# Weight tiles of two modes to a transfer, and a re-ordered last stretch, in a sparse-attention and spectral-mix kernel

## The chip, the cores and the metric

The kernel runs on one core of one Trainium2 chip. The metric is the device time of one execution in microseconds, taken as the median of several runs. A profile is of one execution.

## What is computed

Two layers, one after the other. Attention: 8 batches, 8 heads, 576 rows of 64; the first four heads see a local window of 32 rows, the last four see rows of the same position modulo 32. Then a spectral mix over the rows of the attention's output x (8 x 576 x 512):

```
X = rfft(x, axis=1);  Xr, Xi = real and imaginary part of X[:, :64]
Yr = einsum('bmd,mde->bme', Xr, w_r) - einsum('bmd,mde->bme', Xi, w_i)
Yi = einsum('bmd,mde->bme', Xr, w_i) + einsum('bmd,mde->bme', Xi, w_r)
y = irfft(Y with its first 64 modes set to Yr + i*Yi, n=576, axis=1)
u = x + y
out = u + max(u @ w_ch, 0)
```

`w_r` and `w_i` are 64 x 512 x 512 each, all inputs are float32; each of the 64 modes has weights of its own.

## The kernel before

**Loads.** All of q, k, v, w_r, w_i and w_ch is loaded by POOL (GpSimd), with a cast to float16 in the transfer. POOL is a queue: its transfers are issued in the order of the program, each when the buffer that it writes is free, and at most eight are in flight, since a transfer waits for the landing of the one eight places before it. `w_fetch` (L175) loads the weights of a mode, half of the input channels at a time: part 0 (half 1) for modes 0 to 63, then part 1 (half 0) for modes 0 to 63. One such piece is a tile of 128 partitions x 4 x 512: w_r in partitions 0 to 63, w_i in 64 to 127 (mode 0 has no w_i). Each is a transfer of its own (L190). The pool `pw` has 11 tiles (`NWBUF`); six more pieces (`GUEST`, L169) sit in space that other tiles (X0, Y0, YT) take over later. `w_ch` takes one of the 11 (L197). `load_str` (L214) loads the rows of the strided heads of a batch: 64 partitions by a transfer for each of v, q, k, and for each even batch a small one with partitions 64 to 71 of two batches (L222). `load_loc` (L229) loads those of the local heads.

**Stages.** (1) Strided attention, batch by batch (L742), with loads and weight prefetch at the head of each batch. (2) Local attention (L770), with the 64 modes of part 0 (`mode(0, m)`) spread between its steps. (3) The 64 modes of part 1 (`mode(1, m)`, L837 and L948). `mode` (L532) is 16 matmuls with 16 columns, a weight tile as the stationary operand; after it `w_fetch` asks for the next piece. Beside the modes of part 1 there is a list `work` of 76 pieces: four `w_turn`, and for each batch four `turn` (L578: transposes of x) and five `premix` (L627: four matmuls with 512 columns, x @ w_ch, and four transposes back, with a copy by ACT, L650, and one by DVE, L651). Each `premix` leaves v0 = x @ w_ch and a copy xo of x. `spec` turns 16 finished modes of Y for four batches. (4) The tail: 36 units of 128 rows. `v_rows` (L888) adds irfft(Y) @ w_ch to v0 in PSUM and takes the relu by ACT into `rl` (L897); `u_rows` (L907) makes u, and DVE adds `rl` and writes `osb` (L916), from which SP's queue stores the output. `rl` and `osb` are tiles of `pw` too. `v_early` and `u_early` put v0 and xo into PSUM ahead of that, and `again(n)` (L944) is n matmuls whose result nobody reads.

**The order** of each engine's instructions is that of the program text (`manual_schedule`). In stage 3 the pieces are handed out by hand (L835-L846): with `LATE = 10`, 56 of them evenly beside modes 0 to 50, then two beside each of modes 51 to 60. Then come the early matmuls, and then modes 61, 62 and 63 with nothing between them:

```
for i in range(3):
    if i < 2:
        v_early(i)
    u_early(i)
warm = psum("v")
...
for m in range(NM - 3, NM):
    mode(1, m)
again(2)
spec_last(0)
again(3)
```

Of the kernel before, what the change touches and what calls it, by code (L numbers as in the profile page):

```python
# [10 lines left out]
FP = mybir.dt.float32  # L11
F16 = mybir.dt.float16
# [6 lines left out]
DM = 512  # L19
NM = 64  # L20
# [3 lines left out]
JG = [(0, 6), (6, 11), (11, 16)]  # L24
SCALE = float(1.0 / np.sqrt(D))
NEG = -30000.0
NWBUF = 11


def _host_consts():  # L30
# [49 lines left out]
def kernel(  # L80
# [10 lines left out]
    nc = tc.nc  # L91
# [3 lines left out]
    big = ctx.enter_context(tc.tile_pool(name="big", bufs=1))  # L95
# [5 lines left out]
    def psum_pools(**bufs):  # L101
        pctx.close()
        for n, c in bufs.items():
            pss[n] = pctx.enter_context(
                tc.tile_pool(name="ps_" + n, bufs=c, space=PSUM)
            )

    def psum(kind, half=False):
        if half:
            return pss[kind].tile([128, 1024], F16, tag=kind, name=kind)  # L110
        return pss[kind].tile([128, 512], FP, tag=kind, name=kind)
# [16 lines left out]
    def const_load(eng, *which):  # L128
        for n in which:
            eng.dma_start(cs[n][:, 0 : hosts[names.index(n)].shape[1]], drams[n])  # L130
# [13 lines left out]
    def spectra_tile(n):  # L144
        if n == "X0":
            Xh[0] = big.tile([128, 4, B, 2, NM], F16, tag=n, name=n)
        else:
            YS[n] = big.tile([128, 4, 4, 16, 16], F16, tag=n, name=n)

    xb = [px.tile([128, 11, 256], F16, tag="xb", name="xb") for _ in range(B)]  # L150

    pw = ctx.enter_context(tc.tile_pool(name="pw", bufs=NWBUF))
    actx = ctx.enter_context(ExitStack())
# [3 lines left out]
    ring = pat.tile([128, 12, 2048], F16, name="ring")  # L157
# [8 lines left out]

    GUEST = {3: ("Y0", 0), 4: ("Y0", 1), 5: ("X0", 0), 6: ("X0", 1)}  # L169
    GUEST |= {15: ("YT", 0), 16: ("YT", 1)}  # L170
    guests = {}
    w_tiles = []
    w_chs = {}

    def w_fetch(n=1):  # L175
        for _ in range(n):
            i = len(w_tiles)
            if i >= 2 * NM:
                return
            half, m = 1 - i // NM, i % NM  # L180
            if i in GUEST:
                n, j = GUEST[i]
                if j == 0:
                    guests[n] = big.tile([128, 2, 4, DM], F16, tag=n, name="wt")
                wt = guests[n][:, j]
            else:
                wt = pw.tile([128, 4, DM], F16, tag="w", name="wt")

            for ri, src in enumerate([moe_w_r, moe_w_i] if m else [moe_w_r]):
                nc.gpsimd.dma_start(  # L190
                    wt[ds(64 * ri, 64)],
                    src[m, ds(256 * half, 256), :].rearrange("(p c) e -> p c e", c=4),
                )
            w_tiles.append(wt)

    def w_ch_fetch():
        w_ch = pw.tile([128, 4, DM], F16, tag="w", name="w_ch")  # L197
        nc.gpsimd.dma_start(w_ch, moe_w_ch.rearrange("(c p) e -> p c e", p=128))
        w_chs["n"] = w_ch

# [3 lines left out]
    SRC = {2: v, 0: q, 1: k}  # L204
    SLOT = {2: 0, 0: 1, 1: 2}

    def str_in(b, vi):
        return ring[0:72, 3 * (b % 4) + SLOT[vi], :]
# [2 lines left out]
        t = ring[:, ds(2 * (b % 6), 2), :].rearrange("p n x -> p (n x)")  # L211
        return t[:, ds(1152 * vi, 1152)]

    def load_str(b):  # L214
        for vi in (2, 0, 1):
            nc.gpsimd.dma_start(
                str_in(b, vi)[0:64],
                SRC[vi][b, 4:8].rearrange("h (c r) d -> (h c) (r d)", r=32)[0:64],
            )
            if b % 2 == 0:  # L220
                n = 3 * (b % 4) + SLOT[vi]
                nc.gpsimd.dma_start(  # L222
                    ring[64:72, n : n + 4 : 3, :],
                    SRC[vi][b : b + 2, 4:8].rearrange(
                        "b h (c r) d -> (h c) b (r d)", r=32
                    )[64:72],
                )

    def load_loc(*bs):  # L229
        for b in bs:  # L230
# [301 lines left out]
    def mode(slot, m):  # L532
        half = 1 - slot
        mi, mg = m % 8, m // 8
        if mi == 0:
            ypt[slot] = psum("y")
        yp = ypt[slot]
        yv = yp.rearrange("p (m e x) -> p m e x", m=8, e=4)
        wt = w_tiles[slot * NM + m]
        pr = ds(0, 128 if m else 64)  # L540
        for e in range(4):
            for c in range(4):
                nc.tensor.matmul(  # L543
                    yv[:, mi, e, :],
                    wt[pr, XC[c], ds(128 * e, 128)],
                    Xh[half][pr, c, :, :, m],
                    start=(c == 0),
                    stop=(c == 3),
                )
        if slot or m not in GUEST:  # L550
            w_fetch()
        ends = {7: 8}
        if slot and mg == 7:
            ends = {5: 6, 7: 2}
        if mi in ends:
            n = ends[mi]
            m0 = mi + 1 - n
            part = (
                slice(None),
                slice(None),  # L560
                mg // 2,
                slice(None),
                ds(8 * (mg % 2) + m0, n),
            )
            src = yp.rearrange("p (m e x) -> p e x m", m=8, e=4)[:, :, :, ds(m0, n)]
            if slot == 0:
                if m == 7:
                    spectra_tile("Y0")
                nc.scalar.activation(out=YS["Y0"][part], in_=src, func=ACTF.Copy)
            else:  # L570
                nc.vector.tensor_tensor(
                    out=YS["YT"][part], in0=src, in1=YS["Y0"][part], op=AluOp.add
                )
# [117 lines left out]


    psum_pools(tp=3, sc=3, av=2)
    load_str(0)
    const_load(nc.scalar, "cI", "cM6", "cM5", "cFs")
    load_str(1)
    const_load(nc.sync, "cMl", "cFl", "cA")
    load_str(2)
    w_fetch(2)

    def str_front(b):
        return [
# [19 lines left out]
    first = str_front(0)  # L722
# [16 lines left out]
                )  # L739
    SPLIT = [0, 2, 4, 5, 7, 8, 10]  # L740
    for b in range(B):
        if b < 5:  # L742
            load_str(b + 3)
        load_loc(*[(), (), (), (), (0,), (1, 2), (3,), (4, 5)][b])
        w_fetch([3, 3, 2, 2, 2, 1, 1, 1][b])
        front = str_front(b + 1) if b + 1 < B else loc_front(0)
        for t in range(6):
            str_scores(b, t)
            if b > 0:
                if t < 2:  # L750
                    str_values(b - 1, 4 + t)
                elif t == 2:
                    dft(b - 1, 1)
            if t >= 2:
                str_values(b, t - 2)
            for w in front[SPLIT[t] : SPLIT[t + 1]]:
                w()
        if b == 1:
            nc.vector.memset(PL[:, 0:PS0], 0.0)
# [10 lines left out]
    for b in range(B):  # L770
# [12 lines left out]
        n = 0  # L783
        nm = NMODES[b]
        for mi in range(nm):
            upto = -(-len(work) * (mi + 1) // nm)
            for w in work[n:upto]:
                w()
            n = upto
# [5 lines left out]
    ptr = ctx.enter_context(tc.tile_pool(name="ptr", bufs=1))  # L795
# [36 lines left out]

    n = 0

    LATE = 10  # L835
    first = len(work) - 2 * LATE
    for m in range(NM - 3):  # L837
        mode(1, m)
        if m < NM - 3 - LATE:
            upto = -(-first * (m + 1) // (NM - 3 - LATE))  # L840
        else:
            upto = first + 2 * (m - (NM - 4 - LATE))
        for w in work[n:upto]:
            w()
        n = upto
        if m >= 16 and m % 16 in (4, 8):  # L846
            spec(m // 16 - 1, 0 if m % 16 == 4 else 1)
# [9 lines left out]
    held, vps, ups, rls, osbs = {}, {}, {}, {}, {}  # L857
# [24 lines left out]
    def v_early(i, bank=None):  # L882
        b, t = units[i]
        vps[i] = psum("v") if bank is None else bank
        v0 = v0s[b][:, t, :] if t < 4 else v0h[b // 2]
        nc.tensor.matmul(vps[i], idn, v0, start=True, stop=False)  # L886

    def v_rows(i):  # L888
        b, t = units[i]
        if i not in vps:  # L890
            v_early(i)
        vp = vps.pop(i)
        rows_of(b, t, vp, zzs, False)
        if t % 2 == 0:
            rls[b, t] = rls[b, t + 1] = pw.tile([128, 2, DM], FP, tag="w", name="rl")
        rl = rls[b, t][:, t % 2, :]
        nc.scalar.activation(out=rl, in_=vp, func=ACTF.Relu)  # L897
        if pool_adds(b, t):
            nc.gpsimd.tensor_tensor(out=rl, in0=rl, in1=x_rows(b, t), op=AluOp.add)  # L899

    def u_early(i):
        b, t = units[i]
        ups[i] = psum("u")
        if not pool_adds(b, t):
            nc.tensor.matmul(ups[i], idn, x_rows(b, t), start=True, stop=False)
# [28 lines left out]
                osb,  # L934
            )

    for i in range(3):
        if i < 2:
            v_early(i)
        u_early(i)  # L940
    warm = psum("v")


    def again(n):  # L944
        for i in range(n):
            nc.tensor.matmul(warm, idn, v0s[0][:, 2, :], start=True, stop=True)

    for m in range(NM - 3, NM):  # L948
        mode(1, m)
    again(2)  # L950
    spec_last(0)
    again(3)
    v_early(2, warm)
# [2 lines left out]
    for i in range(len(units)):  # L956
        v_rows(i)
        b, t = units[i]
# [42 lines left out]
```

The softmax here doesn't subtract the row's maximum and nothing guards it: scores larger than these inputs give would overflow.

## Time and profile before

| | |
|---|---|
| median of 7 runs | 437.81 us (437.32 to 440.52) |
| the profiled execution | 437.86 us |
| its span, first to last instruction | 436.1 us |
| mean granted TensorE clock | 0.809 |
| PE, DVE, ACT, POOL busy | 78%, 50%, 43%, 43% |
| weight transfers (L190) | 128 + 126, 256 KB each |
| moved by DMA | 92.20 MB, mean 211 GB/s |
| first output transfer issued | 402.74 us |

How to read it: KB and GB/s are bytes as they are written (float16 for loads); the reads are twice as many. A line of the chain of waits or of the timeline begins with its start and its duration in us; `x16` is the number of instructions that were merged in it; in square brackets is how long the engine had been idle and what released it. In the tables by window the columns are length, busy time of PE, PEld (weight load), DVE, ACT and POOL with their instruction counts, the granted clock, the mean share of the DMA engines, and GB/s. PE busy is the time with a matmul in the pipeline, not its peak use.

### The profile page before, as it was taken

The page shows a single profiled execution, that of the slowest core. Times are in us where ns is not written, and L with a number is a line of the kernel's source. Part 1 is how long each engine was busy: PE and PEld are TensorE (multiplying, and loading weights), DVE is VectorE, ACT ScalarE, POOL GpSimd, SP SyncE. Part 2 cuts the span into 40 slices and gives each one's busy share as a digit, 9 for nine tenths or more (in the row PEclk, how much of TensorE's full clock was granted, in tenths as well). Part 3 has the DMA queues.
Part 4 walks back from the last instruction along what each step waited for, and adds up shares of the span by engine and source line. Part 5 has one row for each costly group of instructions (what it writes and reads, how often), then busy time and mean ns, then how long its engine had stood idle before and what let it go on. Part 6 is the DMA issues. An engine that isn't in the chain of part 4 may idle for free.

```text
span 436.1 us, 12328 instructions
## 1 busy us (share of the span) xinstructions
PE 339.5 (78%) x5289; PEld 244.5 (56%) x5289; DVE 216.2 (50%) x466; ACT 188.4 (43%) x353; POOL 186.6 (43%) x339
## 2 busy tenths in 40 slices
PE   1988878779987789888865567768586859988994
PEld 1867767658766567666743335445344545554441
DVE  2786787945435243252511034354244442764895
ACT  1585777734554345444441202134122312443882
POOL 6545454333344343444343444344344344420883
PEclk9996899956997756685685559598778677999998
DMA  8999999999999999999999999999999999991687
GB/s 173 205 211 210 212 211 212 210 209 211 213 211 213 211 207 211 212 212 212 212 210 213 211 212 211 213 211 212 198 211 212 212 212 211 212 212 36 265 323 280
DMA packets 31095, 92.20 MB, mean 211 GB/s; under 512 B 6145, under 2 KB 7169, under 8 KB 31041
## 3 DMA queue, kind: packets, MB, share of 16 engines
q0 software_dynamic: 26800, 81.29, 94.8%
q1 hardware_dynamic: 3440, 9.46, 5.8%
q10 hardware_dynamic: 800, 0.67, 0.6%
q8 instruction: 42, 0.69, 0.6%
q14 instruction: 13, 0.10, 0.1%
HBM read 163.22 MB, written 9.44 MB: 396 GB/s over the span
## 4 chain that ended last, share of the span: by engine, by line
DMA 56%; PE 27%; DVE 8%; issue 4%; ACT 2%; POOL 1%; DVEq 0%; POOLq 0%
DMA wt<-in_moe_w_i_dram 49%; DMA wt<-in_moe_w_r_dram 5%; PE y L543 3%; PE sc L641 3%; PE sc L510 2%; PE u L684 2%; PE v L684 2%; PE v L886 2%; DVE kz L288 2%; DVE xb L246 2%; DMA ring<-in_v_dram 2%; DMA ring<-in_q_dram 2%; PE tp L320 1%; PE sc L349 1%; PE sc L341 1%
## 5 line engine op out<-in xcount | busy, mean ns | idle before, releaser
L543 PE MATMUL y<-X,wt 128*128 128x16 f16 (+1 forms) x2048 | 82.3, 192 | 56.5 <-DMA wt<-in_moe_w_i_dram 54.7
L190 POOL DMA_DIRECT2D wt<-in_moe_w_r_dram x128 | 65.8, 514 | 118.6 <-DMA wt<-in_moe_w_r_dram 32.0
L543 PEld LDWEIGHTS <-wt 128*128 128x128 f16 (+1 forms) x2048 | 71.9, 103 | 69.9 <-issue 48.0
L190 POOL DMA_DIRECT2D wt<-in_moe_w_i_dram x126 | 64.7, 514 | 68.9 <-DMA wt<-in_moe_w_i_dram 51.0
L650 ACT ACTIVATE v<-sc 128x512 f16<-128x512 f32 x32 | 19.0, 597 | 88.0 <-PE sc L641 87.9
L641 PE MATMUL sc<-w_cp,xT 128*128 128x512 f16 (+1 forms) x160 | 51.6, 452 | 0.5 <-DVE xT L613 0.4
L467 ACT ACTIVATE PL<-sc 128x480 f16<-128x480 f32 (+1 forms) x48 | 27.5, 579 | 42.9 <-PE sc L453 42.4
L651 DVE COPY xo<-tp 128x512 f16<-128x512 f16 x32 | 22.1, 691 | 39.9 <-PE tp L649 39.9
L246 DVE TENSOR_TENSOR xb<-av,rec 90x256 f16<-90x256 f32 (+2 forms) x80 | 36.0, 450 | 2.8
L245 DVE RECIPROCAL rec<-av 90x4 f32<-90x4 f32 (+2 forms) x80 | 14.7, 183 | 41.3 <-PE av L482 29.0
L398 DVE COPY qT<-tp 128x576 f16<-128x576 f16 x16 | 12.0, 758 | 41.8 <-PE tp L391 38.3
L256 ACT ACTIVATE v<-tp 128x640 f16<-128x640 f16 (+1 forms) x24 | 19.4, 808 | 22.7 <-PE tp L425 18.9
L356 ACT ACTIVATE PL<-sc 90x360 f16<-90x360 f32 (+1 forms) x48 | 23.0, 489 | 10.6 <-PE sc L349 9.8
L391 PE MATMUL tp<-cI_s,ring 64*64 64x64 f16 x864 | 26.0, 210 | 1.4 <-issue 0.6
L899 POOL TENSOR_TENSOR rl<-rl,xo 128x512 f32<-128x512 f32 x16 | 18.3, 1156 | 18.3 <-ACT rl L897 17.9
L916 DVE TENSOR_TENSOR osb<-u,rl 128x512 f32<-128x512 f32 x36 | 23.6, 688 | 2.6 <-PE u L684 1.3
L391 PEld LDWEIGHTS <-ring 64*64 64x64 f16 x864 | 20.6, 123 | 6.5 <-issue 4.0
L453 PE MATMUL sc<-qT,kz 128*128 128x160 f16 (+1 forms) x160 | 22.5, 266 | 1.9 <-issue 1.9
L437 PE MATMUL sc<-cMl_s,cI_s 128*128 128x480 f16 (+1 forms) x48 | 22.5, 469 | 1.6 <-ACT X L256 1.6
L281 PE MATMUL tp<-cI_s,ring 72*128 72x72 f16 x256 | 15.0, 207 | 10.8 <-DMA ring<-in_v_dram 7.8
L641 PEld LDWEIGHTS <-xT 128*128 128x128 f16 (+1 forms) x160 | 14.8, 110 | 14.7 <-issue 6.8
L453 PEld LDWEIGHTS <-kz 128*128 128x128 f16 x160 | 16.2, 116 | 12.0 <-issue 9.2
(98 smaller groups left out, 655.3 us busy)
## 6 DMA issues: line engine op xcount, KB each, us to landing
wt<-in_moe_w_r_dram POOLq DMA_DIRECT2D x128, 256.0 KB, 9.4
wt<-in_moe_w_i_dram POOLq DMA_DIRECT2D x126, 256.0 KB, 9.6
out_dram<-osb SPq DMA_DIRECT2D x14, 512.0 KB, 2.7
ring<-in_v_dram POOLq DMA_DIRECT2D x8, 288.0 KB, 10.2
ring<-in_q_dram POOLq DMA_DIRECT2D x8, 288.0 KB, 10.4
ring<-in_k_dram POOLq DMA_DIRECT2D x8, 288.0 KB, 10.7
ring<-in_v_dram POOLq DMA_DIRECT2D x8, 256.0 KB, 8.3
ring<-in_q_dram POOLq DMA_DIRECT2D x8, 256.0 KB, 8.5
```

What stands on the lines that cost most here:

```text
L190: nc.gpsimd.dma_start(wt[ds(64 * ri, 64)], src[m, ds(256 * half, 256), :].rearrange("(p c) e -> p c e", c=4),)
L246: nc.vector.tensor_tensor(out=dst, in0=val.rearrange("p h (q c) -> p h c q", c=4), in1=rec[0:n, 0:pieces] .to_broadcast((n, pieces, 64)) . ...
L256: nc.scalar.activation(out=out, in_=in_, func=ACTF.Copy)
L356: nc.scalar.activation(out=PS[0:n, ds(POFF[t], 4 * n)], in_=scp[0:n, 0 : 4 * n], func=ACTF.Exp, scale=SCALE,)
L391: nc.tensor.transpose(tp[ds(64 * hp, 64), ds(64 * i, 64)], qn[ds(64 * hp, 64), ds(64 * (9 * g + i), 64)], idn[ds(64 * hp, 64), ds(64 * hp, ...
L437: nc.tensor.matmul(scp[:, 0 : n * times].rearrange("p (h x) -> p h x", h=times), idn, mask_rows("cMl", n, times), start=True, stop=False,)
L453: nc.tensor.matmul(scp[:, ds(col, n)], kzs[par][:, hp, ds(s0, 128)], qTs[par][:, ds(s0, n)], start=False, stop=(i == len(todo) - 1),)
L467: nc.scalar.activation(out=dst, in_=src, func=ACTF.Exp, scale=SCALE)
L543: nc.tensor.matmul(yv[:, mi, e, :], wt[pr, XC[c], ds(128 * e, 128)], Xh[half][pr, c, :, :, m], start=(c == 0), stop=(c == 3),)
L641: nc.tensor.matmul(vp[pr, :], xT[:, ch, cols], w_chs["cp"][:, ch, :], start=(ch == 0), stop=(ch == 3),)
L651: nc.vector.tensor_copy(out=xo[pr].rearrange("p (h q c) -> p h q c", h=2, c=4), in_=tp[pr, 0:512].rearrange("p (h c q) -> p h q c", h=2, c=4),
L916: nc.vector.tensor_tensor(out=osb[:, t % 2, :], in0=up, in1=rls[b, t][:, t % 2, :], op=AluOp.add)
```

## The change

1. **Pairs of modes.** A weight tile holds two modes (`[128, 2, 4, 512]`), the pool has 5 of them (before: 11 of one mode), three more sit in the space of Y0, X0 and YT. One transfer brings w_r of both modes, one w_i of both. Single transfers are left for w_i beside mode 0 and for the last four modes of part 1, in the order w_r, w_r, w_i, w_i of a pair. `w_fetch` is called after odd modes. The prefetch ahead of part 0 is 16 pieces (before: 17).
2. **Strided rows.** Batches 2 and 3, 4 and 5, 6 and 7 come in one transfer for each of v, q, k; batches 0 and 1 as before. Batches 4, 5 are asked for at the head of batch 1, 6 and 7 at that of batch 3.
3. **w_ch** has a tile of its own. `rl` no longer uses `pw`, but in turn two tiles with the tag of xT and two of a new tag.
4. **Last six modes.** `LATE` is 12 and the list of pieces ends beside mode 57: 52 pieces beside modes 0 to 45, two beside each of modes 46 to 57. The five early matmuls stand after modes 58 (three) and 59 (two), three `again` after each of modes 60, 61 and 62, two after mode 63.

The core of the diff:

```diff
-NWBUF = 11
+NWBUF = 5
...
-    GUEST = {3: ("Y0", 0), 4: ("Y0", 1), 5: ("X0", 0), 6: ("X0", 1)}
-    GUEST |= {15: ("YT", 0), 16: ("YT", 1)}
+    GUEST = {1: "Y0", 2: "X0", 7: "YT"}
+    w_ch = big.tile([128, 4, DM], F16, name="w_ch")
...
-            for ri, src in enumerate([moe_w_r, moe_w_i] if m else [moe_w_r]):
-                nc.gpsimd.dma_start(
-                    wt[ds(64 * ri, 64)],
-                    src[m, ds(256 * half, 256), :].rearrange("(p c) e -> p c e", c=4),
-                )
-            w_tiles.append(wt)
+            if i // 2 in GUEST:
+                wt = big.tile([128, 2, 4, DM], F16, tag=GUEST[i // 2], name="wt")
+            else:
+                wt = pw.tile([128, 2, 4, DM], F16, tag="w", name="wt")
+            for ri, src in enumerate((moe_w_r, moe_w_i)):
+                dst = wt[ds(64 * ri, 64)]
+                rows = src[m : m + 2, ds(256 * half, 256), :].rearrange(
+                    "m (p c) e -> p m (c e)", c=4
+                )
+                dst = dst.rearrange("p m c e -> p m (c e)")
+                ones = range(2)
+                if ri and not m:
+                    ones = [1]
+                elif i < 2 * NM - 4:
+                    nc.gpsimd.dma_start(dst, rows)
+                    continue
+                for j in ones:
+                    nc.gpsimd.dma_start(dst[:, j], rows[:, j])
+            w_tiles.extend((wt[:, 0], wt[:, 1]))
...
+            two = ring[:, n : n + 4 : 3, :]
+            src = SRC[vi][b - b % 2 : b - b % 2 + 2, 4:8].rearrange(
+                "b h (c r) d -> (h c) b (r d)", r=32
+            )
+            if nb == 2:
+                nc.gpsimd.dma_start(two[0:64], src[0:64])
+            else:
+                nc.gpsimd.dma_start(ring[0:64, n, :], src[0:64, b % 2])
             if b % 2 == 0:
+                nc.gpsimd.dma_start(two[64:72], src[64:72])
...
-        if slot or m not in GUEST:
+        if m % 2 and (slot or m // 2 not in GUEST):
             w_fetch()
...
-        if b < 5:
-            load_str(b + 3)
+        if b in (1, 3):
+            load_str(b + 3, 2)
...
-        w_fetch([3, 3, 2, 2, 2, 1, 1, 1][b])
+        w_fetch([2, 1, 1, 1, 1, 1, 0, 0][b])
...
-    LATE = 10
+    LATE = 12
+    END = NM - 6
...
-            rls[b, t] = rls[b, t + 1] = pw.tile([128, 2, DM], FP, tag="w", name="rl")
+            n = len(rls) // 2 % 2
+            rl = ptr.tile([128, 2, 576], FP, tag="xT" if n else "rl", bufs=2, name="rl")
+            rls[b, t] = rls[b, t + 1] = rl[:, :, 0:DM]
...
-    for m in range(NM - 3, NM):
+    early = [lambda i=i: v_early(i) for i in range(2)]
+    early += [lambda i=i: u_early(i) for i in range(3)]
+    warm = psum("v")
+    for m in range(END, NM):
         mode(1, m)
-    again(2)
+        if m < END + 2:
+            for w in early[3 * (m - END) : 3 * (m - END) + 3]:
+                w()
+        else:
+            again(3 if m < NM - 1 else 2)
     spec_last(0)
```

More of the change, by code (lines that the diff above doesn't have):

```diff
@@ L165 @@
     v16 = [pat.tile([128, 12, 132], F16, name=f"v16_{i}") for i in range(2)]
-    GUEST = {3: ("Y0", 0), 4: ("Y0", 1), 5: ("X0", 0), 6: ("X0", 1)}
-    GUEST |= {15: ("YT", 0), 16: ("YT", 1)}
-    guests = {}
+    GUEST = {1: "Y0", 2: "X0", 7: "YT"}
     w_tiles = []
     w_chs = {}
+    w_ch = big.tile([128, 4, DM], F16, name="w_ch")
     def w_fetch(n=1):
@@ L180, in w_fetch @@
             half, m = 1 - i // NM, i % NM
[L181 to L185, printed above, removed]
-            else:
-                wt = pw.tile([128, 4, DM], F16, tag="w", name="wt")
-            for ri, src in enumerate([moe_w_r, moe_w_i] if m else [moe_w_r]):
-                nc.gpsimd.dma_start(
-                    wt[ds(64 * ri, 64)],
-                    src[m, ds(256 * half, 256), :].rearrange("(p c) e -> p c e", c=4),
-                )
-            w_tiles.append(wt)
+            if i // 2 in GUEST:
+                wt = big.tile([128, 2, 4, DM], F16, tag=GUEST[i // 2], name="wt")
+            else:
+                wt = pw.tile([128, 2, 4, DM], F16, tag="w", name="wt")
[3 more added lines that the diff above has]
+                    "m (p c) e -> p m (c e)", c=4
+                )
+                dst = dst.rearrange("p m c e -> p m (c e)")
[8 more added lines that the diff above has]
+            w_tiles.extend((wt[:, 0], wt[:, 1]))
     def w_ch_fetch():
-        w_ch = pw.tile([128, 4, DM], F16, tag="w", name="w_ch")
         nc.gpsimd.dma_start(w_ch, moe_w_ch.rearrange("(c p) e -> p c e", p=128))
@@ L212, in loc_in, with load_str @@
         return t[:, ds(1152 * vi, 1152)]
-    def load_str(b):
+    def load_str(b, nb):
         for vi in (2, 0, 1):
-            nc.gpsimd.dma_start(
-                str_in(b, vi)[0:64],
-                SRC[vi][b, 4:8].rearrange("h (c r) d -> (h c) (r d)", r=32)[0:64],
-            )
+            n = 3 * (b % 4) + SLOT[vi]
+            two = ring[:, n : n + 4 : 3, :]
+            src = SRC[vi][b - b % 2 : b - b % 2 + 2, 4:8].rearrange(
+                "b h (c r) d -> (h c) b (r d)", r=32
+            )
+            if nb == 2:
+                nc.gpsimd.dma_start(two[0:64], src[0:64])
+            else:
+                nc.gpsimd.dma_start(ring[0:64, n, :], src[0:64, b % 2])
             if b % 2 == 0:
[L221 to L226, printed above, removed]
-                )
+                nc.gpsimd.dma_start(two[64:72], src[64:72])
     def load_loc(*bs):
@@ L693 @@
     psum_pools(tp=3, sc=3, av=2)
-    load_str(0)
+    load_str(0, 1)
     const_load(nc.scalar, "cI", "cM6", "cM5", "cFs")
-    load_str(1)
+    load_str(1, 1)
     const_load(nc.sync, "cMl", "cFl", "cA")
-    load_str(2)
-    w_fetch(2)
+    load_str(2, 2)
+    w_fetch()
     def str_front(b):
@@ L833 @@
     n = 0
-    LATE = 10
+    LATE = 12
+    END = NM - 6
     first = len(work) - 2 * LATE
-    for m in range(NM - 3):
+    for m in range(END):
         mode(1, m)
-        if m < NM - 3 - LATE:
-            upto = -(-first * (m + 1) // (NM - 3 - LATE))
+        if m < END - LATE:
+            upto = -(-first * (m + 1) // (END - LATE))
         else:
-            upto = first + 2 * (m - (NM - 4 - LATE))
+            upto = first + 2 * (m + 1 - (END - LATE))
         for w in work[n:upto]:
@@ L935, in u_rows @@
             )
[L937 to L941, printed above, removed]
     def again(n):
```

## The prediction

> **What bounds the kernel now.** I read the slices of the page first, then the chain of waits, then the DMA issues, and last the timeline of the final 40 us.
>
> ```profile
> PEclk9996899956997756685685559598778677999998
> DMA  8999999999999999999999999999999999991687
> GB/s 173 205 211 210 212 211 212 210 209 211 213 211 213 211 207 211 212 212 212 212 210 213 211 212 211 213 211 212 198 211 212 212 212 211 212 212 36 265 323 280
> ...
> q0 software_dynamic: 26800, 81.29, 94.8%
> ...
> DMA 56%; PE 27%; DVE 8%; issue 4%; ACT 2%; POOL 1%; DVEq 0%; POOLq 0%
> ...
> wt<-in_moe_w_r_dram POOLq DMA_DIRECT2D x128, 256.0 KB, 9.4
> wt<-in_moe_w_i_dram POOLq DMA_DIRECT2D x126, 256.0 KB, 9.6
> ```
>
> From slice 2 to slice 36 (10.9 to 392 us) the DMA engines are full at one level, 211 to 213 GB/s written: an input stream, and no compute engine is near full over that stretch. The time is the end of this stream plus a tail in which the output is made. In the chain, ordered by time, the stream looks like this:
>
> ```profile
> 247.31 9.63 DMA wt<-in_moe_w_i_dram
> 257.22 9.63 DMA wt<-in_moe_w_i_dram
> 267.13 9.62 DMA wt<-in_moe_w_i_dram
> ```
>
> Each link is one transfer from issue to landing, and links start 9.91 us apart. POOL keeps eight transfers in flight and waits for the one eight places back, so 9.91/8 = 1.239 us is the time of one 256 KB transfer. The packet records of the trace split it: on one DMA engine four 4096-byte packets start 0.305 us apart, then one 4-byte packet (the semaphore write) holds the engine for 0.020 us: 4 x 0.305 + 0.020 = 1.240. The end of the stream:
>
> ```profile
> 387.19 0.52 POOL L190 DMA_DIRECT2D wt<-in_moe_w_i_dram  x1 [0.48 <-DMA wt<-in_moe_w_i_dram]
> ...
> 396.82 0.56 DVE L571 TENSOR_TENSOR YT<-y,Y 128x384 f16<-128x384 f32 x1 [1.84 <-PE y L543]
> 397.43 1.12 PE L543 MATMUL y<-X,wt 128*128 128x16 f16 x32 [0.72 <-DVE YT L571]
> ...
> 398.94 1.04 PE L878 MATMUL y<-w_ch,YT 128*128 128x512 f16 x4
> ```
>
> The last transfer, issued at 387.19, lands at 396.95 by its semaphore. Mode 63 is the second half of the 32 matmuls: it starts at 397.91 and ends at 398.5. So PE is 0.96 us late at the end of the stream; in the DMA-bound stretch it usually starts a mode 0.14 us after the landing. After 398.5 come 37.6 us in which nothing of the change lies on the path but the clock that PE has. For that, three windows of the middle and three of the end (PE, PEld, DVE, ACT and POOL busy, then clock, DMA share, GB/s):
>
> ```profile
> 225.00:262.00 37.00, 21.68 (x322) 14.41 (x323) 6.58 (x16) 6.40 (x13) 14.93 (x29) 0.50 1.07 211
> 354.00:365.00 11.00, 7.64 (x90) 4.85 (x91) 3.01 (x8) 0.76 (x2) 4.71 (x10) 0.54 1.06 212
> 365.00:378.00 13.00, 11.54 (x160) 7.69 (x158) 8.19 (x17) 5.38 (x10) 5.59 (x11) 0.99 1.06 212
> 392.00:398.50 6.50, 4.99 (x70) 3.24 (x69) 2.15 (x4) 1.19 (x2) 0.00 (x0) 1.00 0.36 70
> 398.50:405.40 6.90, 6.54 (x33) 2.65 (x30) 3.96 (x8) 4.39 (x9) 1.20 (x2) 1.00 0.21 80
> 405.40:430.00 24.60, 24.60 (x118) 11.19 (x116) 22.37 (x36) 20.51 (x36) 21.58 (x19) 1.00 0.81 308
> ```
>
> Where PE is busy 59% (21.68 of 37.00) it has half the clock; at 89% it has all of it. The tail runs at full clock and PE is full in it (24.60 of 24.60): a half clock there costs time.
>
> **What the Trainium skill says.** "DMA: Bandwidth & Descriptors", section "Why a DMA increments its semaphore by 16 and not by 1": on the GpSimd path all 16 engines post a +1 whatever the shape. The trace agrees: queue 0 has 5232 four-byte packets, 16 for each of 303 transfers and 32 for the 12 small ones of L222. The same page, "Anatomy of one DMA", calls the semaphore write about one cycle, essentially free, and the fixed 2 us of a transfer completion latency. Here it is 0.020 us of every engine; I take the trace. The 2 us are hidden by eight in flight. "TensorE: Matmul & The Clock Gate", Part 1: half clock after an idle window of some 3.4 us, full again after a busy one, windows free-running. The clock record changes only between 0.50 and 1.00, after multiples of 3.41 us; it agrees.
>
> **The change part by part.**
>
> *Joined transfers.* Weights: before 128 + 126 = 254 transfers. After, 62 of the 64 pairs take two transfers (the two pairs with mode 0: one joined, one single), the last two pairs four: 124 + 8 = 132, so 122 fewer. Strided rows: 24 + 12 before; after 6 + 9 joined + 12 = 27, so 9 fewer. Bytes and 4096-byte packets are the same. 131 x 0.020 us = 2.62 us less on each engine. Since the engines that end last have no gap in the stream (each lands a transfer every 1.24 us to the end), all of it comes off the end: 396.95 becomes 394.3. Bounds: 0 if the joined access is split again below the program, 3 us if a boundary costs a little more than its packet.
>
> *POOL's 131 issues less*, 0.51 us each, are worth nothing: POOL is waiting for DMA or for a buffer before nearly every one.
>
> *Fewer and larger buffers.* Five pairs are ten modes; a buffer comes free after its second mode, and then four pairs, 8 x 2.46 = 19.7 us of transfers, stand before it. PE's lag behind a landing is at most 3.5 us once the lead of the first modes is used up, so the stream doesn't run dry. At the start 16 modes are loaded ahead, not 17; pair 8 can be issued after mode 1 (99.1 us), when by the landings of before 11 us are still queued (to 110 us), pair 9 after mode 7 (108.1), with work queued to 115. No gap; cost 0. If the cover were gone, each us of gap is a us. The rows of batches 2 and 3 come together: row 2 of k lands at some 23.6 us, not 20.3; its transposes come after 24.
>
> *w_ch at home, rl elsewhere.* The pool keeps five buffers for osb, and rl gets four. From the times of before: a sixth osb is written at least 4.2 us after the output of the first has landed, and a fifth rl 1.2 us or more after the last read of the first. No wait; cost 0, at worst some tenths.
>
> *No pieces beside the last six modes.* The 24 late pieces go from modes 51-60 to 46-57, with their PE, ACT (0.60 us) and DVE (0.69 us) instructions; no DMA moves. In the trace a mode with two pieces takes PE 2.7 us and the stream brings one in 2.46, so PE falls behind: 12 modes lose some 2 to 3 us, which modes 58 and 59 (0.5 us each and five 512-column matmuls of 0.216 us) win back. Mode 63 then starts 0.14 us after its landing, not 0.96: 0.82 us gained. The nine added warming matmuls are 9 x 0.216 = 1.9 us of PE in waits; after mode 62 they just fit (0.5 + 0.65 in 1.24 us).
>
> *The clock at the end.* The last four modes are single transfers in the order r62, r63, i62, i63, so mode 62 lands 1.24 us before the end and mode 61 4.96 before. PE has modes 58 to 61 and their fillers done 2.5 to 3.4 us before the end and then nothing until mode 62: 1.3 to 2.2 us idle in a window of 3.4, so 60 to 40% busy, near where the clock is lost (it is lost at 59%, kept at 89%). Unknown, bounded from both sides: 0 if it is kept. It isn't below 0, since the clock of before is 1.00 to the end. If it is lost, the tail starts at half clock for 3 to 5 us: 1.5 to 2.5 us of PE time, of which 0.36 was idle (6.54 of 6.90), and the fillers after mode 62 take 1.3 us in place of 0.65 and delay mode 63 by up to 0.55: 1.2 to 2.7, I take 1.8. I take "kept", narrowly: PE's lag into mode 58 is more likely nearer 3 us than 2, and fillers stand between the modes.
>
> Sum: 436.1 - 2.62 - 0.82 = 432.7 us of span; 1.76 us lie around the span (437.86 of the profiled run), so 434.4. The median of the runs (437.81) is 0.05 below the profiled run, which changes nothing.
>
> **The rivals.** *The clock is lost* near the end: 434.4 + 1.8 = 436.2. For it: 59% busy has half clock; against: fillers, and a filled stretch until mode 59. *Only the order helps*: the joined access comes out as as many semaphore writes as before; the time is 437.81 - 0.82 = 437.0. Against it: the 12 small strided transfers of L222, which already join two batches, are one instruction each, though with twice the semaphore packets. *Slower*: the joined weight transfer reads rows of two modes in turn, 1 MB apart, and its packets slow down. There are 1016 weight packets for each engine; at 0.305 + x us they cost 1016x, so from x = 0.0034 us (1.1%) on the gain of 3.4 is gone, and at 0.312 us the time is 434.4 + 7.1 = 441.5. Against it: nearly all 4096-byte packets take 0.322 to 0.324 us in the records, strided rows and weights alike, so they look bound by the engine. *A residue* for a stream that runs dry at 99-120 us or a wait in the tail: about 438.
>
> **How the numbers follow.** Forecast 0.49; clock lost 0.32; order alone 0.06; slower packets 0.07; residue 0.06. The forecast's own range is 433.4 to 435.4 (boundary cost, where an instruction fetch falls). The range 433.4 to 437.1 takes in the lost clock and the order alone, and leaves out the slower packets, the residue and half of the rest's edges. This kernel's measurement tells 0.3% (1.3 us) from no change: faster means below 436.5. Faster: 0.49 + three quarters of the lost clock = 0.73; same: the rest of it (0.08), order alone (0.06), half of the residue (0.03) = 0.17; slower 0.10.
>
> **What would show it.** Right: about 184 load transfers; joined ones landing 2.46 us apart, the last at about 394.3; mode 63 within 0.2 us of it; 37.6 us after its end; clock 1.00 in the last windows. Wrong: packets over 0.305 us apart; a gap on the slowest engines; a PE wait on i62 followed by 0.427 us matmuls; DVE or ACT waiting for an output DMA.

## The result and the profile after

The changed kernel takes 434.6 us (median of 12 runs, 434.03 to 435.41) against 438.06 us for the kernel before (31 runs): a ratio of 0.9918, with a 95% interval of 0.9905 to 0.9932, or some 3.6 us. The forecast was 434.4 us. The profiled execution has a span of 432.4 us (before 436.1). The sum was right; the experiments below show that its two terms don't stand by themselves as the prediction had them.

The page of the kernel after, slices, queue, chain and issues:

```profile
PEclk9999899959896857868885558697868877999998
DMA  8999999999999999999999999999999999992787
GB/s 173 204 211 213 213 212 214 211 210 211 214 213 214 214 213 214 213 214 214 213 212 213 214 214 214 213 213 214 213 213 213 213 215 214 213 199 42 268 319 287
...
q0 software_dynamic: 24704, 81.28, 94.9%
...
DMA 73%; PE 18%; DVE 2%; issue 2%; ACT 2%; POOL 1%; DVEq 0%; POOLq 0%
...
wt<-in_moe_w_r_dram POOLq DMA_DIRECT2D x62, 512.0 KB, 19.0
wt<-in_moe_w_i_dram POOLq DMA_DIRECT2D x60, 512.0 KB, 19.4
```

The stream is still one flat level, now at 213 to 215 GB/s over most slices where it was 211 to 213. Queue 0 has 2096 packets fewer (26800 - 24704), which is 131 x 16: exactly the semaphore writes of 131 transfers, and the bytes are the same. DMA's share of the chain went from 56% to 73% and PE's from 27% to 18%, but not at the end: in the first 120 us the chain has 99.5 us of DMA where it had 14.3, and in another profile of the changed kernel (changed again, below) it has 21.8 there and 54% in all. In the chain, by time, a link is now one joined transfer, eight in flight, and takes twice as long, with no loss of rate (8 joined transfers in 19.66 us):

```profile
255.68 19.38 DMA wt<-in_moe_w_i_dram
275.34 19.38 DMA wt<-in_moe_w_i_dram
```

Ahead of the tail the chain leaves the stream well before the stream ends, and from there on runs through PE and the engines that it waits for. First the chain before, then after:

```profile
357.46 9.63 DMA wt<-in_moe_w_i_dram
367.22 0.65 PE y L543 x16
```

```profile
335.52 19.38 DMA wt<-in_moe_w_i_dram
355.03 0.64 PE y L547 x16
```

Before, that stretch began with mode 51, the first with two pieces; after, it begins with mode 46, again the first with two pieces.

The end of the stream in the timeline of PE (the last load, issued at 384.67, lands at 394.30 by its semaphore; before 396.95):

```profile
388.42 0.65 PE L547 MATMUL y<-X,wt 128*128 128x16 f16 x16
...
392.11 0.64 PE L547 MATMUL y<-X,wt 128*128 128x16 f16 x16
392.58 0.81 PE L948 MATMUL v<-v,cI_s 128*128 128x512 f16 x3
393.46 0.64 PE L547 MATMUL y<-X,wt 128*128 128x16 f16 x16
393.94 0.81 PE L948 MATMUL v<-v,cI_s 128*128 128x512 f16 x3
394.58 0.64 PE L547 MATMUL y<-X,wt 128*128 128x16 f16 x16
...
395.61 1.04 PE L883 MATMUL y<-w_ch,YT 128*128 128x512 f16 x4
```

Mode 58 starts at 388.42, mode 63 at 394.58, 0.28 us after its landing (before 0.96). The tail from the first `spec_last` matmul (395.61, before 398.94) follows in the same steps. The windows of the end:

```profile
374.00:389.50 15.50, 13.96 (x185) 9.30 (x183) 11.65 (x24) 8.77 (x15) 2.58 (x5) 1.00 1.01 201
389.50:395.20 5.70, 5.63 (x95) 3.76 (x95) 0.56 (x1) 0.00 (x0) 0.00 (x0) 1.00 0.35 70
395.20:402.10 6.90, 6.54 (x33) 2.69 (x31) 3.96 (x8) 4.41 (x9) 1.22 (x2) 1.00 0.21 80
402.10:427.00 24.90, 24.75 (x118) 11.18 (x116) 22.71 (x37) 20.49 (x36) 21.55 (x19) 1.00 0.81 309
```

PE is busy for 5.63 of the last 5.70 us of the modes and has the whole clock into the tail. From the first write of `osb` to the last is 28.60 us in both kernels, so the new homes of `rl` and `osb` cost nothing. The span is 3.64 us shorter (432.44 against 436.08): 3.33 is gained by the start of the tail, 0.3 lies after the last write of `osb`, in the last store.

### The profile page after: what moved, and what is told of

It reads as the page before. It is cut to its first block, busy times and chain, and to the rows that moved or that the text cites. A ratio compares the mean times of both kernels' runs of the same rounds, so it can differ in the third digit from the quotient of the medians.

```text
span 432.4 us, 12081 instructions
## 1 busy us (share of the span) xinstructions
PE 334.4 (77%) x5298; PEld 241.2 (56%) x5298; DVE 215.2 (50%) x466; ACT 188.0 (43%) x353; POOL 128.9 (30%) x208
## 3 DMA queue, kind: packets, MB, share of 16 engines
q0 software_dynamic: 24704, 81.28, 94.9%
## 4 chain that ended last, share of the span: by engine, by line
DMA 73%; PE 18%; DVE 2%; issue 2%; ACT 2%; POOL 1%; DVEq 0%; POOLq 0%
DMA wt<-in_moe_w_i_dram 51%; DMA ring<-in_v_dram 8%; DMA ring<-in_k_dram 6%; DMA wt<-in_moe_w_r_dram 5%; DMA ring<-in_q_dram 4%; PE sc L645 3%; PE y L547 2%; PE u L688 2%; PE v L688 2%; PE v L891 2%; PE tp L653 1%; PE u L912 1%; ACT zz L260 1%; PE tp L324 1%; DVE xT L597 1%
## 5 line engine op out<-in xcount | busy, mean ns | idle before, releaser
L196 POOL DMA_DIRECT2D wt<-in_moe_w_r_dram x62 | 36.4, 587 | 143.4 <-PE y L547 56.9
L196 POOL DMA_DIRECT2D wt<-in_moe_w_i_dram x60 | 35.2, 587 | 70.6 <-DMA wt<-in_moe_w_i_dram 57.6
L645 PE MATMUL sc<-w_cp,xT 128*128 128x512 f16 (+1 forms) x160 | 50.7, 440 | 1.8 <-DVE xT L617 1.8
L597 DVE COPY xT<-tp 128x512 f16<-128x512 f16 x16 | 11.0, 688 | 28.1 <-PE tp L591 16.2
L260 ACT ACTIVATE kz<-tp 64x360 f16<-64x360 f16 (+1 forms) x32 | 19.0, 594 | 10.2 <-PE tp L395 8.8
```

The costliest lines, as they stand in the source:

```text
L196: nc.gpsimd.dma_start(dst, rows)
L260: nc.scalar.activation(out=out, in_=in_, func=ACTF.Copy)
L645: nc.tensor.matmul(vp[pr, :], xT[:, ch, cols], w_chs["cp"][:, ch, :], start=(ch == 0), stop=(ch == 3),)
```

## The experiments

Each was timed in five rounds beside the kernel before. The profiles give four numbers for each: the load transfers, when the last weight landed, how long after that mode 63 began, and how long from there to the first write of `osb` (4.11 us at full clock). After that all have 28.4 to 28.6 us of tail to the last `osb`. The ratios are of medians, and each profile is of one run: those of split by rows (440.22 us, median 436.98), split by mode (439.02, median 437.92) and pieces four earlier (436.46, median 435.31) are of runs more than 1 us above their medians.

| kernel | loads | last landing | mode 63 after it | to the first `osb` | ratio to before, interval |
|---|---|---|---|---|---|
| before | 315 | 396.95 | 0.96 | 4.11 | 1 |
| changed | 184 | 394.30 | 0.28 | 4.11 | 0.9918 (0.9905 to 0.9932) |
| changed again | 184 | 394.37 | 1.05 | 4.11 | 0.9922 (0.99 to 0.9943) |
| changed beside | 184 | 394.83 | 0.40 | 4.10 | 0.993 (0.9911 to 0.9949) |
| joined only | 184 | 394.01 | 4.68 | 4.11 | 0.9995 (0.998 to 1.001) |
| order only | 315 | 396.18 | 0.14 | 5.51 | 1.0014 (1.0001 to 1.0027) |
| split by mode | 306 | 397.27 | 0.55 | 4.89 | 0.9996 (0.9984 to 1.0008) |
| split by rows | 306 | 396.54 | 3.61 | 4.11 | 0.9981 (0.9968 to 0.9995) |
| no fillers | 184 | 394.70 | 0.14 | 5.52 | 0.9958 (0.9939 to 0.9977) |
| pieces four earlier | 184 | 395.07 | 0.13 | 5.70 | 0.9943 (0.9921 to 0.9965) |
| order, more fillers | 315 | 396.79 | 0.13 | 4.11 | 0.9963 (0.995 to 0.9977) |
| joined, even pieces | 184 | 394.43 | 0.43 | 4.11 | 0.9924 (0.9905 to 0.9943) |
| before, even pieces | 315 | 395.81 | 0.14 | 6.73 | 0.9994 (0.9978 to 1.0009) |
| even and fillers | 178 | 394.42 | 0.05 | 4.11 | 0.9905 (0.9887 to 0.9923) |

### The two halves of the change, each alone

Joined only: the changed kernel with the end of the kernel before.

```diff
-    LATE = 12
-    END = NM - 6
+    LATE = 10
...  (pieces beside modes 51 to 60, early matmuls after 60, nothing between 61, 62, 63)
```

> The changed kernel with the end of the kernel before: pieces two to a mode beside modes 51 to 60, the five early matmuls after mode 60, nothing between modes 61, 62 and 63. What is left of the change is the joined transfers and the buffers. Theory (the stream's end is set by 4-byte packets of 0.020 us, 131 fewer): 2.6 us below the kernel before, the last weight landing near 394.3 us, mode 63 about 1 us after it. Rival (the time went with the order of the end alone, the joined transfers are hidden): within 0.5 us of the kernel before.

Order only: the kernel before with the end of the changed one.

```diff
-    LATE = 10
+    LATE = 12
+    END = NM - 6
...  (pieces beside modes 46 to 57, early matmuls after 58 and 59, fillers after 60 to 62)
```

> The kernel before with the last stretch of the changed one: pieces end beside mode 57, early matmuls after modes 58 and 59, fillers after 60 to 62; transfers and buffers as before. Theory: the last landing stays near 397 us and mode 63 starts 0.1 to 0.3 us after it in place of 0.96: 0.7 to 0.8 us below the kernel before. Rival (the order is the larger part): 2 us or more below it. Rival (clock lost, since the single transfers leave PE idle between modes): 0.5 to 2 us above it.

Neither gains anything: 0.9995 and 1.0014. Joined only does what the theory says to the stream, which ends at 394.01, but not to the time. PE's timeline of that kernel:

```profile
385.32 0.65 PE L547 MATMUL y<-X,wt 128*128 128x16 f16 x16
...
389.31 1.64 PE L645 MATMUL sc<-w_cp,xT 128*128 128x512 f16 x4
...
392.09 0.64 PE L547 MATMUL y<-X,wt 128*128 128x16 f16 x16
392.57 1.03 PE L645 MATMUL sc<-w_cp,xT 128*128 128x512 f16 x4
...
395.81 0.39 PE L890 MATMUL v<-v,cI_s 128*128 128x512 f16 x1 [0.79 <-DVE xoh L655]
...
396.90 0.59 PE L547 MATMUL y<-X,wt 128*128 128x16 f16 x16
398.21 1.12 PE L547 MATMUL y<-X,wt 128*128 128x16 f16 x32 [0.72 <-DVE YT L575]
```

Mode 60 starts at 392.09, then come its two pieces, a wait of 0.79 us for a copy by DVE, the early matmuls, mode 61, a wait of 0.72 us for DVE, and modes 62 and 63 from 398.21 on, all with their weights landed. In the kernel before the same modes start at 397.43. Two ends met there: that of the stream, and that of PE's backlog of pieces (PE's work that still waits when its weights have landed). Taking 2.9 us off one left the other.

Two things explain, as far as one profile of each kernel can, why the backlog didn't end sooner with the stream. A pair lands as a whole, so its first mode waits for the second: mode 54 landed at 374.26, only 0.30 us sooner than alone in the kernel before (374.56), mode 55 2.74 sooner, and PE began mode 54 0.14 us after its landing and is behind from there on. And PE lost its clock once on the way, so that four matmuls at 389.31 took 1.64 us, not 1.03:

```profile
387.16:390.57 3.41, 3.41 (x27) 1.76 (x28) 0.69 (x1) 0.60 (x1) 0.00 (x0) 0.50 0.61 121
```

At mode 58 this kernel was 0.67 us ahead of the kernel before (385.32 against 385.99), at mode 60 0.78 us behind (392.09 against 391.31), and so it still is at mode 63. So in this profile the half clock took 1.45 us, which the kernel before didn't lose there; without it some 0.7 us of the 2.9 would have come through, by this account.

Order only moves mode 63 to 0.14 us after its landing, and loses it again at once (its PE timeline, then the window of the loss):

```profile
394.31 0.81 PE L940 MATMUL v<-v,cI_s 128*128 128x512 f16 x3
396.32 0.64 PE L543 MATMUL y<-X,wt 128*128 128x16 f16 x16 [1.20 <-DMA wt<-in_moe_w_i_dram]
...
397.60 1.91 PE L879 MATMUL y<-w_ch,YT 128*128 128x512 f16 x4
```

```profile
396.50:399.90 3.40, 3.40 (x27) 1.70 (x24) 0.29 (x1) 0.35 (x1) 0.00 (x0) 0.51 0.03 5
```

PE idled 1.20 us before mode 63 and 0.63 before mode 62; the clock was 0.51 for the next 3.4 us, four matmuls took 1.91 us in place of 1.04, and the first `osb` came 5.51 us after mode 63, not 4.11. This is the first rival of the prediction, the lost clock, in another kernel.

### Is it the number of transfers?

Two kernels issue the joined weight transfers of the changed kernel as two again, into the same pair tiles:

```diff
-                elif i < 2 * NM - 4:
-                    nc.gpsimd.dma_start(dst, rows)
-                    continue
```

> The changed kernel with each joined weight transfer issued again as two, one for each mode, into the same pair tile: 122 more transfers, all else equal. Theory (a semaphore packet holds each engine 0.020 us): 122 x 0.020 = 2.4 us above the changed kernel. Rival (the gain is from reading two modes' rows in turn, or from larger transfers in flight): with only eight transfers in flight the bytes in flight halve; if that matters the time rises by more than 3 us; if only the order of the end matters, it doesn't rise.

```diff
-                    nc.gpsimd.dma_start(dst, rows)
+                    for z in (0, 32):
+                        nc.gpsimd.dma_start(dst[z : z + 32], rows[z : z + 32])
```

> The changed kernel with each joined weight transfer cut in two by partitions (32 rows of both modes each): as many transfers as when cut by mode, but rows of the two modes are still read in turn. Theory (only the number of transfers counts): 2.4 us above the changed kernel, the same as the cut by mode to 0.5 us. Rival (the way in which HBM is read counts): the two cuts differ by more than 1 us.

Both give most or all of the gain back: 0.9996 and 0.9981, so 3.4 and 2.8 us above the changed kernel, a little more than the 2.4 expected. In the profiles the landing moves by 2.97 and 2.24 us. The two cuts read HBM in different order. Their intervals overlap, but their medians (437.92 and 436.98 us of 22 runs each) differ by 0.9 us, close to the 1 us that was named as the sign of the rival. So the count of transfers accounts for most of it, and a smaller share of the way of reading is not excluded. Both cuts also halve the bytes in flight, so these two runs don't tell the number of transfers from their size. More than the landing is in these times: in the first the clock dipped (4.89 us to the first `osb`), in the second half-clock windows at 371 and 385 us made PE's backlog longer (mode 63 at 3.61 us after its landing).

### What keeps the clock

The changed kernel without fillers after modes 60 to 62, and with its pieces four modes earlier:

```diff
-            again(3 if m < NM - 1 else 2)
+            again(0 if m < NM - 1 else 2)
```

> The changed kernel without the nine filler matmuls after modes 60, 61 and 62 (the two after mode 63 stay). Theory (PE was still 4 us behind at mode 58, so it is busy up to mode 61 anyway; without fillers it idles some 2 us before mode 62): the clock is at the edge; if it is lost, half clock at the start of the tail, 512-column matmuls at 0.43 us there, and 1 to 2.5 us above the changed kernel; if it is kept, within 0.3 us of it. Rival (the fillers only cost, since mode 63 starts behind them): 0.1 to 0.2 us below it.

```diff
+    LAST2 = END - 4
...  (END replaced by LAST2 in the three lines that hand out pieces: two a mode beside 42 to 53)
```

> The changed kernel with the two-a-mode pieces beside modes 42 to 53 in place of 46 to 57; modes 54 to 57 stand alone, all else equal. Theory (the backlog of pieces is what keeps PE busy until mode 61): PE has caught up before mode 58, idles over 2 us before mode 62 in spite of the fillers, and the clock is lost near the end: 1.2 to 2.7 us above the changed kernel. Rival (the fillers alone keep the clock): within 0.3 us of it, and mode 63 starts 0.1 to 0.3 us after its landing.

No fillers is 1.7 us above the changed kernel by the ratios (0.9958 against 0.9918), pieces four earlier 1.1 us (0.9943, with an interval that overlaps that of the changed kernel, so the times alone don't show this loss). In both, mode 63 is closer to its landing than in the changed kernel (0.14 and 0.13), and in both the tail starts at half clock. The window after the modes without fillers, and in the kernel with earlier pieces:

```profile
395.10:398.50 3.40, 3.40 (x24) 1.62 (x21) 0.31 (x2) 0.37 (x1) 0.00 (x0) 0.50 0.00 0
```

```profile
396.10:399.50 3.40, 3.40 (x12) 1.46 (x12) 0.99 (x4) 0.37 (x1) 0.00 (x0) 0.50 0.00 0
```

So in these profiles the clock of the changed kernel's order is held by fillers and backlog together: without the backlog, three fillers a mode are too few. It is not the only way to hold it: joined, even pieces (below) has no fillers between its last modes, and its profile has the whole clock from 384.10 us on, into the tail.

### Does the order pay alone when the clock is kept, and is it the bunching that binds?

The order-only kernel with longer fillers:

```diff
-            again(3 if m < NM - 1 else 2)
+            again({NM - 4: 3, NM - 3: 6, NM - 2: 8, NM - 1: 2}[m])
```

> The kernel before with the order of the changed one, as in the order-only run, but with 3, 6 and 8 filler matmuls after modes 60, 61 and 62 in place of three each, so that PE is busy up to mode 63. Theory (the order alone is worth 1 to 1.6 us at mode 63, and the lost clock took it back): the clock stays at 1.00 into the tail, and the time is 1 to 1.6 us below the kernel before. Rival (the fillers delay mode 63 or something else takes the gain): no faster than the order-only run, within 0.3 us of the kernel before or above it.

```profile
394.79 1.89 PE L940 MATMUL v<-v,cI_s 128*128 128x512 f16 x8
396.92 0.64 PE L543 MATMUL y<-X,wt 128*128 128x16 f16 x16 [0.24 <-DMA wt<-in_moe_w_i_dram]
397.40 0.59 PE L940 MATMUL v<-v,cI_s 128*128 128x512 f16 x2
397.95 1.04 PE L879 MATMUL y<-w_ch,YT 128*128 128x512 f16 x4
```

0.9963, or 1.6 us below the kernel before: the eight fillers cover the wait to 0.24 us, `spec_last` takes 1.04 us again. Eight more fillers than the order-only kernel has turn no gain into 1.6 us.

The other way round, the pieces spread evenly, with the old end (early matmuls after mode 60, no fillers between the last modes), on the joined transfers and on the kernel before:

```diff
-    LATE = 10
+    LATE = 0
```

> The joined-only kernel with its 76 pieces spread evenly beside modes 0 to 60, none bunched at two to a mode; early matmuls after mode 60 and nothing between 61, 62 and 63, as before. Theory (joined alone gained nothing because the bunched pieces make PE the bound of the last 30 us): with the backlog gone mode 63 starts within 0.6 us of the last landing near 394.3, and the time is 2 to 3.5 us below the kernel before. Rival (the joined transfers gain only with the early matmuls and fillers placed between the last six modes): no faster than the joined-only kernel. If the clock is lost at the end, up to 2 us of the gain goes again.

> The kernel before with one number changed: its pieces spread evenly beside modes 0 to 60, none bunched. Theory (before, PE and the stream ended together; with the backlog gone only the stream is left): mode 63 some 0.1 to 0.6 us after the last landing near 396.8, 0.4 to 0.9 us below the kernel before if the clock is kept. Rival (PE alone was the bound before): 2 us or more below it.

On joined transfers this one number brings 0.9924, within the interval of the whole change. PE's timeline of it:

```profile
393.07 0.59 PE L547 MATMUL y<-X,wt 128*128 128x16 f16 x16
394.38 1.12 PE L547 MATMUL y<-X,wt 128*128 128x16 f16 x32 [0.72 <-DVE YT L575]
...
395.89 1.04 PE L882 MATMUL y<-w_ch,YT 128*128 128x512 f16 x4
```

Compared with joined only, modes 62 and 63 start at 394.38, not 398.21: the bunched pieces (with the clock that was lost among them) were the bound, not the missing fillers. On the kernel before, the same number gains nothing (0.9994): mode 63 is at 0.14 us after a landing at 395.81, and PE had waited 1.26 us for it, so the tail ran cold for longer than in any other kernel:

```profile
398.00:402.00 4.00, 4.00 (x14) 1.67 (x13) 1.17 (x3) 0.63 (x2) 0.00 (x0) 0.50 0.01 2
```

### A try at a better version

The changed kernel with even pieces, fillers that reach the last landing, and six transfers fewer:

```diff
-    LATE = 12
+    LATE = 0
-            again(3 if m < NM - 1 else 2)
+            again({NM - 4: 4, NM - 3: 12, NM - 2: 2, NM - 1: 2}[m])
...  (load_loc: batches 1 and 2, and 4 and 5, in one transfer for each of v, q, k)
```

> A try at a better version, from what the runs showed: the changed kernel with its pieces spread evenly beside modes 0 to 57, fillers 4, 12, 2 and 2 after modes 60 to 63 so that PE is busy up to the last landing, and the rows of two local batches (1 and 2, 4 and 5) in one transfer for each of v, q, k: 6 transfers fewer. Theory: 0.12 us from the transfers, 0.15 us at mode 63, the clock at 1.00 in the tail in every run: 0 to 0.5 us below the changed kernel, which can hardly be measured. Rival (long fillers or the even spread cost something): above it.

434.45 us, ratio 0.9905 (0.9887 to 0.9923). The changed kernel was run again beside it:

> The changed kernel on the same chip as the two beside it, for comparison: 3.2 to 3.8 us below the kernel before.

434.78 us, 0.993 (0.9911 to 0.9949). The intervals overlap, so a gain over the changed kernel is not shown. Its six runs lie between 433.73 and 434.84, those of the changed kernel between 433.5 and 437.45, but only 4 of these 15 are above 435, so six runs are too few to show a smaller spread. One more repetition, beside the two kernels with more fillers and with even pieces:

> The changed kernel once more, on the same chip as the two beside it, so that they can be compared with it: 3.2 to 3.8 us below the kernel before, clock 1.00 at the end.

gave 434.6 us, 0.9922 (0.99 to 0.9943).

## Why the prediction was right, and where its steps were not

**The transfers.** 184 loads, 131 fewer, as counted. The landing moved by 2.65 us in the two profiles (term: 2.62). That close a match is partly luck: with 315 loads the four profiles have 396.95, 396.18, 396.79 and 395.81 (mean 396.4), with 178 or 184 the eight have 394.01 to 395.07 (mean 394.5), so the mean step is 1.9 us and one landing scatters by about 1 us. That fewer and larger transfers end the stream sooner is shown, by an amount known to some 0.7 us; that the 4-byte packets alone do it is argued from their 0.020 us, since no run changed their number without the size of the transfers.

**"All of it comes off the end"** was the step that failed as it was put. It is true of the stream and false of the time: joined only gives 0.9995. The prediction took one stream to bound the kernel up to its end, with no compute engine near full, read PE's lateness from mode 63, 0.96 us, and took it for all that PE had to give. Its own window had PE busy for 11.54 of 13.00 us at 365 to 378, the chain left the stream at 367, and PE, whose lag was put at 3.5 us at most, was 4.26 us late at mode 61. That a backlog of 4 us had shrunk to 1 us at the last landing meant that both ends fell within 1 us of each other, so that neither a shorter stream nor a shorter backlog alone could give more than about that. That the pair holds back its first mode was not in the prediction.

**The order's 0.82 us** is the mis-sized term for the same reason. Beside the old transfers it is worth 1.6 us if the clock is kept; beside the joined ones the difference between joined only and the whole change is 0.9995 to 0.9918, some 3.4 us. The sum came out because the two terms describe the same end, which mode 63 marks in both kernels: the stream's end plus a small lateness.

**PE's backlog** at mode 58 was put at 2 to 3 us; it was 4.04 (388.42 against a landing at 384.38). (The late pieces of the kernel before are 20, two beside each of modes 51 to 60, not 24.) Modes 58 and 59 won only part of it back: 2.94 us were left at mode 60, 0.33 at mode 62. That error was luck, since the backlog filled the gap before mode 62 in which 1.3 to 2.2 us of idle time were forecast.

**The clock** was given 0.49 against 0.32 to be kept, at a price of 1.2 to 2.7 us. It was kept; and five kernels in which PE idled 1.2 to 1.4 us before mode 62 or 63, or had no fillers, lost it, at 0.8 to 2.6 us to the first `osb` in their profiles. The low-clock rows of the trace (PE busy 59%, half clock) had hinted at it. The Trainium skill ("TensorE: Matmul & The Clock Gate", Part 1) speaks of windows of some 3.4 us, and the clock records agree: these losses last 3.4 or 6.8 us. It calls the window that loses the clock an idle one; in the order-only kernel it was not, for PE was busy for 1.58 of the 3.41 us ahead of the loss:

```profile
393.13:396.54 3.41, 1.58 (x28) 0.94 (x28) 0.08 (x1) 0.00 (x0) 0.00 (x0) 1.00 0.37 72
```

**At nothing** were costed the buffers of five pairs, the later rows, and `rl` and `osb`: the stream shows no pause (the slices stay at 210 to 215 GB/s from 22 to 378 us), and the tail has the same 28.60 us. POOL's issue of a joined transfer takes 0.59 us, not 0.51; it waits before nearly every one.

**Left open**: why single runs of one kernel differ by 1 to 3 us. The changed kernel has three profiles. In changed again the clock was half from 380.61 to 384.02 and mode 63 came 1.05 us after its landing, not 0.28; in changed beside the last landing was 0.53 us later. So the clock windows and the landing each moved the end by half a microsecond or more, but no run above 435.1 us of this kernel was profiled, and what makes 437 is not shown.

## What to carry to other kernels

When a stream and an engine end together, look at the engine's lateness over its last several steps, not at the last one, and at where the chain of waits leaves the stream: if the lateness is falling from 4 us to 1, two bounds are about to meet, and cutting either alone gives almost nothing. Then judge edits as pairs: here 0 and 0 made 3.6 us. And an engine that has become punctual has begun to wait, so ask what its clock does in the wait; here fillers up to the landing kept it.

## What was not expected of the hardware

With eight transfers of 512 KB in flight, not 256 KB, the DMA engines drift apart further: the first engine finishes the last load at 388.01 and the last at 394.30, 6.3 us apart (before 392.96 and 396.95, 4.0 apart). It is so in every profile: 2.7 to 4.0 us apart in the six kernels with 306 or 315 loads, the two split ones among them, and 6.2 to 6.6 in the eight profiles with 178 or 184. The end of the stream is the end of its slowest engines; the flat mean rate doesn't show this. Between the two sets the eight engines that finish first gained 4.9 us in the mean and the eight that finish last 2.2. The 131 packets of 0.020 us (2.6 us) come near the second number; what gave the first engines twice as much is open.
